# One more mirrored block of a symmetric score matrix turned by the DMA, and a third raw tile for V

## The chip, the cores and the metric

The kernel runs on one core of one Trainium2 chip. The metric is the device time of one launch in microseconds (us): the median of three runs of the kernel before is 2292.09 us (2291.48 to 2294.13). One further execution was taken with the profiler; all times inside the kernel come from it.

## The reference

Two stages follow each other. The first is an attention without softmax over 8 batches of 2496 rows; the second a mixture of 8 experts, in which each row goes to the one expert with the largest gate logit.

```
scores = (1/S) * z @ z.T              # per batch, S = 2496, z is [S, 64]
attn   = maximum(scores, 0) ** 2
x      = u * (attn @ v)               # v, u are [S, 256]
e      = argmax(x @ w_gate)           # per row, 8 experts
out    = softmax(x @ w_gate)[e] * (maximum(x @ w1[e], 0) @ w2[e])
```

`z @ z.T` is symmetric, and so is `attn`: the block of rows A and columns B is the transpose of the block of rows B and columns A.

## The kernel before, in words

**Tiling of the attention.** The 2496 rows of a batch are cut into five chunks of queries, 0 to 3 of 512 rows and 4 of 448. Keys go in ten pairs of 128-row tiles, `kp` = 0 to 9; two pairs make one chunk of keys, `cc = kp // 2`. A step is one (batch b, chunk c, pair kp). In each step `scores` (L255) makes a tile of 256 keys by up to 512 queries of `attn`, split into a rounded high part `hi` and a remainder `lo`, and `weighted` (L338) multiplies V into it: twelve matmuls of 128x128 by 128x512 (L346, L348, L349; V's high part by hi, V's high part by lo, V's low part by hi), ten in the last pair. `scores` of a step is written three steps ahead of its `weighted`. The order of a chunk's ten pairs comes from `order_of`.

**How a tile of scores comes about.** There are three ways.
- Blocks on or right of the diagonal (cc >= c) are computed: four matmuls (L309, L310) into PSUM, Relu and Square on ACT (L318, L319), the cast to `hi` (L320) and the subtraction to `lo` (L322) on DVE. Blocks right of the diagonal are also kept in one of six `slot` tiles, since they are needed again, mirrored, in chunk cc.
- Blocks left of the diagonal turned by TensorE: when the mirrored block is due, eight 128x128 float32 transposes per step (L281) bring it from the slot into PSUM, ACT copies it to `hi` (L282), DVE subtracts for `lo` (L283).
- Blocks left of the diagonal turned by the DMA: when the block is first computed (into a `tf` tile, of which there are three, rather than into the slot), ACT and DVE each copy one 16-bit half of every float into a `th` tile (L333, L334; three `th` tiles), and SyncE issues one DMA transpose of 512 KB from it into the slot (L335). When the mirrored block is due, ACT and DVE put the halves together again (L266, L267), and `hi` and `lo` are made from that (L268, L269).

`by_dma(c, cc)` (L251) chooses between the last two. Of the ten mirrored blocks of a batch, the four of chunk 4 go over TensorE, and of the other six that of chunks 0 and 3 does too; five go over the DMA. In chunk 3 the pairs 0 and 1 are that sixth block.

**Order within a chunk.** `order_of` (L228) lets the pairs right of the diagonal that the DMA will turn alternate with those that it won't. For chunk 0 of every batch but the first the order is 0, 2, 6, 3, 7, 4, 8, 5, 9, 1. Chunk 0 of the first batch goes in the natural order, 0 to 9.

**V.** A pair of V is fetched by SyncE into a `vr` tile (L137; two such tiles), then split into high and low parts by ACT (L142) and DVE (L143). The V of the next batch is fetched and split during chunk 4, one pair a step in the order in which the next chunk 0 will use them: `fetch_v` of place j and `split_v` of place j - 1 at step j (L877 to L883), the last split at the first step of the next chunk 0. In the first batch `fetch_v` runs two pairs ahead.

**What sets the order of instructions.** The program hands the instructions to a scheduler that plans each engine's order at compile time from the order in the source, dependences and free tiles. What is handed to `pinned` is kept behind the last instruction of each engine so far. Each engine, and SyncE with its DMA issues, then works through its list in order.

**Beside the steps.** At the end of a chunk `gate_x` (L363) forms x from the accumulators and splits it on DVE (L369, L379, L380); in the steps behind it a list of background work makes gate logits (L401), turns x into rows by four DMA transposes of 128 KB (L388, L389, L393), chooses experts, and stores rows and row lists. The experts' stage follows the attention (from about 1392 us in the trace; L779, L802, L805) and is not touched, but for one buffer count.

**Start.** The first matmuls only warm TensorE up: 8, then 4, then 8 of them read a tile named `lp` (L153). The tile `sd` holds raw integers for six constants (iota, L195, cast to float at L208), and later a block of the diagonal.

## Time and profile before

| | |
|---|---|
| median of three runs | 2292.09 us (2291.48 to 2294.13) |
| the profiled execution | 2294.91 us |
| its span, first to last instruction | 2293.2 us |
| granted TensorE clock, mean | 0.998 |
| PE, DVE, ACT busy | 2278.8, 1660.4, 1371.2 us |

The profile names engines PE (TensorE matmul), PEld (its weight loads), DVE (VectorE), ACT (ScalarE), POOL (GpSimd) and SP (SyncE, which issues most DMAs). L281 is line 281 of the kernel before. Matmuls overlap in the pipe, so the duration of one is longer than the distance to the next one; what a group of them costs the engine is read from the distance between starts. A name such as tf<-ps_s tells the tile written and the tile read.

The batches 2 to 6 look alike in the trace, about 172 us each. The part below uses batch 3: its chunks begin, by the first matmul of `weighted`, at 531.9, 569.1, 604.1, 636.4 and 671.5 us, and batch 4 begins at 704.0 us.

### The profile page before, as it was taken

The page shows a single profiled execution, that of the slowest core. Times are in us where ns is not written, and L with a number is a line of the kernel's source. Part 1 is how long each engine was busy: PE and PEld are TensorE (multiplying, and loading weights), DVE is VectorE, ACT ScalarE, POOL GpSimd, SP SyncE. Part 2 cuts the span into 40 slices and gives each one's busy share as a digit, 9 for nine tenths or more (in the row PEclk, how much of TensorE's full clock was granted, in tenths as well). Part 3 has the DMA queues.
Part 4 walks back from the last instruction along what each step waited for, and adds up shares of the span by engine and source line. Part 5 has one row for each costly group of instructions (what it writes and reads, how often), then busy time and mean ns, then how long its engine had stood idle before and what let it go on. Part 6 is the DMA issues. An engine that isn't in the chain of part 4 may idle for free.

```text
span 2293.2 us, 33793 instructions
## 1 busy us (share of the span) xinstructions
PE 2278.8 (99%) x12448; PEld 1937.2 (84%) x12448; DVE 1660.4 (72%) x2963; ACT 1371.2 (60%) x1867; POOL 614.3 (27%) x626
## 2 busy tenths in 40 slices
PE   9999999999999999999999999999999999999998
PEld 7888888888888888888888888888888888888887
DVE  8868868868878868868878867765575666657554
ACT  7747647647647647647647645454565655646554
POOL 1110110110110110110110244553454444445322
PEclk9999999999999999999999999999999999999999
DMA  5536635635626536635635668566667548557620
GB/s 154 102 65 119 117 60 122 119 60 121 119 61 121 119 60 121 120 58 123 120 62 100 111 136 181 153 149 155 158 184 155 178 129 202 142 147 193 154 88 29
DMA packets 421086, 278.92 MB, mean 122 GB/s; under 512 B 355820, under 2 KB 377850, under 8 KB 411696
## 3 DMA queue, kind: packets, MB, share of 16 engines
q1 hardware_dynamic: 389520, 157.59, 37.3%
q0 software_dynamic: 31392, 119.10, 18.1%
q8 instruction: 99, 1.62, 0.4%
q14 instruction: 75, 0.61, 0.1%
HBM read 149.79 MB, written 43.43 MB: 84 GB/s over the span
## 4 chain that ended last, share of the span: by engine, by line
PE 95%; ACT 1%; issue 1%; DMA 1%; DVE 1%; POOL 0%; SPq 0%; POOLq 0%; DVEq 0%; ACTq 0%
PE ph L779 19%; PE acc L349 15%; PE acc L346 15%; PE acc L348 14%; PE y L802 12%; PE y L805 6%; PE ps_s L309 4%; PE ps_s L310 4%; PE ps_s L281 3%; PE pt L401 1%; DMA vr<-in_v_dram 1%; PE ps_s L315 1%; ACT tf L319 0%; ACT tf L318 0%; POOL out_dram L818 0%
## 5 line engine op out<-in xcount | busy, mean ns | idle before, releaser
L349 PE MATMUL acc<-thi,t 128*128 128x512 f32 (+1 forms) x1600 | 615.2, 386 | 0.7 <-DVE t L143 0.7
L346 PE MATMUL acc<-thi,t 128*128 128x512 f32 (+1 forms) x1600 | 604.2, 392 | 0.0
L348 PE MATMUL acc<-tlo,t 128*128 128x512 f32 (+1 forms) x1520 | 585.8, 386 | 1.6 <-DVE tlo L322 1.6
L784 DVE SCALAR_TENSOR_TENSOR t<-ph,t 128x512 fp32r<-128x512 f32 (+1 forms) x328 | 221.3, 676 | 233.7 <-ACT t L783 230.8
L779 PE MATMUL ph<-thi,t 128*128 128x512 f32 (+2 forms) x1248 | 377.4, 360 | 0.0
L783 ACT ACTIVATE t<-ph 128x512 fp32r<-128x512 f32 (+1 forms) x328 | 193.3, 590 | 295.3 <-PE ph L779 283.5
L349 PEld LDWEIGHTS acc<-thi,t 128*128 128x128 f32 x1600 | 300.2, 188 | 56.3 <-DVE t L143 1.4
L346 PEld LDWEIGHTS acc<-thi,t 128*128 128x128 f32 x1600 | 299.6, 188 | 50.6
L348 PEld LDWEIGHTS acc<-tlo,t 128*128 128x128 f32 x1520 | 285.7, 188 | 53.5 <-DVE tlo L322 4.2
L479 POOL DMA_INDIRECT lst<-toks,posi x160 | 179.2, 1120 | 473.4 <-DVE posi L471 427.9
L802 PE MATMUL y<-t,t 128*128 128x512 f32 x1062 | 301.3, 392 | 0.0
L779 PEld LDWEIGHTS ph<-thi,t 128*128 128x128 f32 x1248 | 225.8, 189 | 27.6
L779 PE MATMUL ph<-tlo,t 128*128 128x512 f32 (+2 forms) x624 | 224.9, 360 | 0.0
L802 PEld LDWEIGHTS y<-t,t 128*128 128x128 f32 x1062 | 190.0, 188 | 31.6 <-issue 0.2
L818 POOL DMA_INDIRECT out_dram<-tf,lfidx x136 | 141.1, 1038 | 263.2 <-DVE tf L816 230.7
L805 PEld LDWEIGHTS y<-t,t 128*128 128x128 f32 x1062 | 174.2, 188 | 28.7
L805 PE MATMUL y<-t,t 128*128 128x256 f32 x1062 | 182.7, 280 | 0.0
L310 PE MATMUL ps_s<-t,t 128*128 128x512 f32 (+1 forms) x480 | 178.9, 376 | 0.0
L318 ACT ACTIVATE tf<-ps_s 128x1024 f32<-128x1024 f32 (+2 forms) x129 | 117.2, 909 | 76.7 <-PE ps_s L310 47.5
L383 POOL MEMSET rows<- 128x64 int32 x40 | 9.9, 251 | 557.0 <-DMA xrows<-rows 263.5
L714 POOL DMA_INDIRECT rows<-xrows,lfidx x136 | 142.7, 1049 | 57.0 <-issue 35.0
L320 DVE CAST thi<-tf 128x1024 fp32r<-128x1024 f32 (+2 forms) x129 | 79.5, 620 | 88.4 <-ACT tf L319 81.8
(251 smaller groups left out, 4032.9 us busy)
## 6 DMA issues: line engine op xcount, KB each, us to landing
vr<-in_v_dram SPq DMA_DIRECT2D x80, 256.0 KB
xrows<-rows SPq DMA_DIRECT2D x32, 544.0 KB
u<-in_ut_dram SPq DMA_DIRECT2D x32, 512.0 KB
zr<-in_zt_dram SPq DMA_DIRECT2D x38, 256.0 KB
u<-in_ut_dram SPq DMA_DIRECT2D x8, 448.0 KB
xrows<-rows SPq DMA_DIRECT2D x8, 408.0 KB
rows<-th SPq DMA_TRANSPOSE x160
lst<-toks,posi POOLq DMA_INDIRECT x160
```

What stands on the lines that cost most here:

```text
L310: nc.tensor.matmul(ps[:, i, m:n], lhsT=hl_k, rhs=lh_q[:, m:n], start=False, stop=True)
L346: nc.tensor.matmul(acc[d][:, :n], lhsT=vh, rhs=hi[:, i, :n], start=first and i == 0, stop=False)
L348: nc.tensor.matmul(acc[d][:, :n], lhsT=vh, rhs=lo[:, i, :n], start=False, stop=False)
L349: nc.tensor.matmul(acc[d][:, :n], lhsT=vl, rhs=hi[:, i, :n], start=False, stop=last and i == 1)
L479: i = nc.gpsimd.indirect_dma_start(out=lst1, out_offset=bass.IndirectOffsetOnAxis(ap=posi[:m, j:j + 1], axis=0), in_=toks[:m, col + j:col ...
L714: nc.gpsimd.indirect_dma_start(out=xg[:, s, :], out_offset=None, in_=src, in_offset=bass.IndirectOffsetOnAxis(ap=lists[which]["idx"][:, s, ...
L779: nc.tensor.matmul(o, lhsT=w1[:, part, dd, fs], rhs=xx[:, dd, :n], start=p == 0, stop=p == 5)
L783: nc.scalar.activation(hh[:, :m], ph[:, :m], AF.Relu)
L784: nc.vector.scalar_tensor_tensor(hl[:, :m], ph[:, :m], 0.0, hh[:, :m].bitcast(F32), op0=ALU.max, op1=ALU.subtract)
L802: nc.tensor.matmul(y, lhsT=h[:, cs], rhs=w2[:, f % 2].rearrange("p i d -> p (i d)"), start=f == 0, stop=False)
L805: nc.tensor.matmul(y[:, 0:D], lhsT=h[:, cs], rhs=w2[:, f % 2, 0, :], start=False, stop=f == NF - 1)
L818: d = nc.gpsimd.indirect_dma_start(out=out, out_offset=bass.IndirectOffsetOnAxis(ap=lists[which]["idx"][:, s, t:t + 1], axis=0), in_=yo[:, ...
```

## The change: what it does

It has four edits.
1. `by_dma` is true for chunks 0 and 3 as well: six of ten mirrored blocks are turned by the DMA.
2. In `order_of`, in chunk 0, three pairs that the DMA will turn come first, and only then do the two kinds alternate. The order becomes 0, 2, 3, 4, 5, 8, 6, 9, 7, 1.
3. `vr` gets a third tile (also where the tile lists of the experts' stage use that name). In chunk 4, step 0 fetches two places of the next batch's V and step j place j + 1; the splits stay where they were.
4. The warm-up matmuls read the `sd` tile, so the tile `lp` is gone. Its 2 KB per partition are the size of one `vr` tile.

```
-        vraw[b, kp] = sb.tile([P, 2, D], F32, name="vr", bufs=2)
+        vraw[b, kp] = sb.tile([P, 2, D], F32, name="vr", bufs=3)
...
-    warm = sb.tile([P, 2, QC], U16, name="lp", tag="lp")[:, 0].bitcast(BF16)
+    warm = ring_sd().rearrange("p s r -> p (s r)")[:, 0:QC // 2].bitcast(BF16)
...
-            mixed = []
+            mixed = [ways[0].pop(0) for _ in range(0 if c else 3)]
...
-        return c < cc < NC_ - 1 and (c, cc) != (0, 3)
+        return c < cc < NC_ - 1
...
-                r["tl", h] = sb.tile([P, 2, D], F32, name="vr", bufs=2).rearrange("p a d -> p (a d)")[:, 0:SMALL]
+                r["tl", h] = sb.tile([P, 2, D], F32, name="vr", bufs=3).rearrange("p a d -> p (a d)")[:, 0:SMALL]
...
-            fetch_v(b + 1, order_of(b + 1, 0)[j])
+            for i in ((0, 1) if j == 0 else (j + 1,) if j < NKP - 1 else ()):
+                fetch_v(b + 1, order_of(b + 1, 0)[i])
```

## The prediction

> **What bounds the kernel now.** I read the page first (engines, then the chain), then the groups of instructions, then the busy time by stretches of one batch.

> ```profile
> span 2293.2 us, 33793 instructions
> PE 2278.8 (99%) x12448; PEld 1937.2 (84%) x12448; DVE 1660.4 (72%) x2963; ACT 1371.2 (60%) x1867; POOL 614.3 (27%) x626
> PE 95%; ACT 1%; issue 1%; DMA 1%; DVE 1%; POOL 0%; SPq 0%; POOLq 0%; DVEq 0%; ACTq 0%
> ```

> PE is busy for 99% of the span and is 95% of the chain that ended last. A busy PE could still be a PE that waits a little, so the groups come next: busy, mean of one, then idle time before them and who ended it.

> ```profile
> L348 PE MATMUL acc<-tlo,t 128*128 128x512 f32 (+1 forms) x1520 | 585.8, 386 | 1.6 <-DVE tlo L322 1.6
> L281 PE MATMUL ps_s<-ident,s 128*128 128x128 f32 x640 | 86.0, 274 | 0.0
> L283 DVE TENSOR_TENSOR tlo<-ps_s,thi 128x896 fp32r<-128x896 f32 (+1 forms) x80 | 89.3, 1117 | 59.1 <-ACT thi L282 58.3
> L282 ACT CAST thi<-ps_s 128x896 fp32r<-128x896 f32 (+1 forms) x80 | 74.2, 928 | 111.9 <-PE acc L349 60.0 <-PE ps_s L281 51.8
> L266 ACT COPY tf<-s 128x1024 uint16<-128x1024 uint16 x80 | 105.2, 1359 | 13.7 <-DVE tlo L269 10.3 <-ACT thi L282 2.5 <-DMA s<-th 0.8
> L268 ACT CAST thi<-tf 128x1024 fp32r<-128x1024 f32 x80 | 82.7, 1052 | 59.9 <-PE acc L349 44.8 <-DVE tlo L269 8.8 <-DVE tf L267 4.2
> L267 DVE COPY tf<-s 128x1024 uint16<-128x1024 uint16 x80 | 57.7, 754 | 0.0
> L269 DVE TENSOR_TENSOR tlo<-tf,thi 128x1024 fp32r<-128x1024 f32 x80 | 97.8, 1223 | 32.4 <-ACT thi L268 31.1
> L333 ACT COPY th<-tf 128x1024 uint16<-128x1024 uint16 x80 | 83.9, 1049 | 0.7
> L334 DVE COPY th<-tf 128x1024 uint16<-128x1024 uint16 x80 | 55.2, 691 | 0.0
> ```

> The main matmuls hardly ever wait: the largest group that waits for DVE lost 1.6 us in the whole run. Work taken from PE in the attention should therefore shorten the run, as long as the work put on ACT, DVE and the DMA stays in their idle time. Where that idle time is, the five chunks of batch 3 show (stretch, length, then busy of PE, PEld, DVE, ACT, POOL, clock, DMA share, GB/s):

> ```profile
> 531.90:569.10 37.20, 37.20 (x193) 30.25 (x192) 31.63 (x53) 29.46 (x34) 5.30 (x5) 1.00 0.70 136
> 569.10:604.10 35.00, 35.00 (x185) 28.86 (x184) 30.37 (x59) 25.76 (x30) 5.37 (x5) 1.00 0.61 119
> 636.40:671.50 35.10, 35.10 (x206) 29.26 (x204) 25.53 (x47) 16.31 (x18) 6.07 (x7) 1.00 0.23 63
> 671.50:704.00 32.50, 32.50 (x196) 29.82 (x195) 21.40 (x34) 17.69 (x23) 2.29 (x4) 1.00 0.49 96
> 528.90:550.80 21.90, 21.90 (x123) 17.90 (x123) 21.62 (x40) 14.61 (x19) 2.00 (x2) 1.00 0.77 180
> 13.00:45.00 32.00, 31.83 (x140) 25.70 (x138) 29.48 (x43) 27.22 (x32) 0.00 (x0) 1.00 0.70 156
> ```

> PE is full in each. Chunk 3 (third row) has much room: ACT idles 18.8 us, DVE 9.6 us. Chunk 0 (first row) has little, and its first part (fifth row) none: DVE works 21.62 of 21.90 us there. Chunk 0 of batch 0 (last row) is nearly as tight. The change puts work into all three places, and that is the whole question.

> **The change part by part.** *Transposes on PE that go.* Two steps of chunk 3 in each of 8 batches lose their eight transposes: 16 groups, 128 of the 640 instructions. What a group costs PE is read from the chain, where each piece runs until the next begins.

> ```profile
> 627.04 0.87 PE ps_s L281 x8
> 632.00 0.23 PE acc L349
> ```

> A group advances PE by 0.87 us, a plain matmul by 0.23. So 16 x 0.87 = 13.9 us go from the engine that bounds the run. The row of 274 ns for one transpose is its time in the pipe; eight of them by that would be 2.2 us, not 0.87. [...]

> *Putting the block together in chunk 3.* Each of the 16 steps changes L282 and L283 for L266, L267, L268 and L269. ACT gets 1359 + 1052 - 928 = 1483 ns more, DVE 754 + 1223 - 1117 = 860 ns more; per chunk 3.0 us and 1.7 us. Six such steps then follow each other, each with only its twelve matmuls on PE, 12 x 0.23 = 2.8 us, against 2.4 us on ACT and 2.0 us on DVE, and `gate_x` besides. I cost it at nothing: it is covered by 18.8 us and 9.6 us of idle time, and ACT in that stretch waits for PE rather than the reverse, as in this row of the timeline:

> ```profile
> 641.82 1.05 ACT L268 CAST thi<-tf 128x1024 fp32r<-128x1024 f32 x1 [4.25 <-PE acc L349]
> ```

> Were that cover gone, it would cost up to 8 x 3.0 = 24 us.

> *Taking the halves in chunk 0.* Two more steps a batch run L333 (1.05 us on ACT), L334 (0.69 us on DVE) and one DMA transpose; Relu and Square are as long as before, only into `tf` rather than a slot. Per chunk 0 that is 2.1 us of ACT and 1.4 us of DVE, and by the new order four such steps stand among the first five in place of two. DVE decides. In batches 1 to 7 it has 5.6 us idle in the chunk, but 0.3 us in the first part, so taken alone the addition would cost PE between nothing (the idle time behind absorbs it) and 1.4 us a batch. Against it works the third edit. In that same first part DVE still splits four pairs of V:

> ```profile
> 528.90:550.80 21.90, 2.78 (x4) 1.00 0.77 180
> 507.83 3.86 SPq L137 DMA_DIRECT2D vr<-in_v_dram  x2
> 516.85 5.16 SPq L393 DMA_TRANSPOSE rows<-th  x4
> 522.11 1.00 SPq L137 DMA_DIRECT2D vr<-in_v_dram  x2
> 526.37 5.63 SPq L137 DMA_DIRECT2D vr<-in_v_dram  x3
> ACT t L142 <- DMA vr<-in_v_dram: 55.8, 20, 5.2
> 198.35 0.50 PE L348 MATMUL acc<-tlo,t 128*128 128x512 f32 x1 [1.42 <-DVE tlo L322]
> ```

> The first row is the busy time of L143 alone. They come so late because with two tiles a fetch waits for the split two places earlier, and SyncE, working in order, then stands in four transposes of rows for 5.2 us; ACT waits for V 20 times, 55.8 us in all. With three tiles each fetch can be issued one split sooner, ahead of those transposes, and the splits move into chunk 4, where DVE idles 11.1 us and ACT 14.8 us. I take two splits moved out of the first part: -2 x 0.69 against +2 x 0.69, net nothing, with +1.4 us a batch (no split moves) and -1.4 us (all four do) as ends. A gain beyond nothing can only come from waits that are there, and those are few: the 1.6 us above, nearly all of it at 198 us, in chunk 0 of batch 1 (last row).

> *SyncE and the DMA.* Each added transpose occupies SyncE and the rings; behind it in SyncE's list stand fetches of V, u and z and the stores of rows. For its price, the one transpose of the stretch from 560 to 569 us:

> ```profile
> 559.96 3.54 SPq L335 DMA_TRANSPOSE s<-th  x1
> q1 hardware_dynamic: 2526, 0.63, 76.8%
> GB/s 224 177 17 10 7 72 85 38 26 38 30 74 10 33 93 155 284 289 291 290 291 265 74 0 0 0 0 0 0 0 0 0 0 0 0 0 0 0 0 0
> ```

> At the top rate, some 290 GB/s, 0.52 MB take 1.8 us; by the share of the stretch (76.8% of 9 us for 0.63 MB, some of it rows) 5.7 us. I take 3.5 us, SyncE's own time on it. Two more bring chunk 0 from 0.70 x 37.2 = 26.0 us of DMA to 33.0, under 37.2, so I cost it at nothing; u, z and the rows have until the end of the chunk, and V will have been fetched earlier. If that cover is gone, ACT stands before a `th` tile still being read (second rival). [...]

> *Chunk 0 of batch 0.* Pairs 6 and 7 gain the halves in natural order, and no split of V can move to an earlier chunk. DVE has 2.5 us idle in 32 and ACT is held by V behind SyncE's transposes:

> ```profile
> 31.03 2.88 SPq L335
> 34.01 3.00 DMA vr<-in_v_dram
> 37.04 0.62 ACT t L142
> ```

> The third tile lets V be fetched a step sooner, which answers the two transposes more in SyncE's list. I take the DVE work at full price, 1.4 us; the ends are 0 and, if V comes late by one SyncE transpose and its landing, 2.9 + 3.0 = 5.9 us.

> *The start.* The constants' integers share a tile with the warm-up, so POOL's iota and DVE's casts wait for warm-up matmuls. Now they lie in DVE's wait for the first z:

> ```profile
> 1.69 0.10 DVE L208 CAST e_down<-sd 128x8 f32<-128x8 int32 x1
> 3.63 0.51 DVE L130 CAST t<-x 64x512 fp32r<-64x512 f32 x1 [0.39 <-DMA x<-in_zt_dram]
> 4.31 0.20 DVE L208 CAST tno<-sd 128x23 f32<-128x23 int32 x1
> ```

> From 1.69 on, and again up to 4.51, they take some 2.0 us. Moved behind, they fall into the tight first chunk: between 0 and 2.0 us; I take 1.0.

> *Sum.* -13.9 + 0 (chunk 3) + 0 (chunks 0 of batches 1 to 7) + 1.4 + 1.0 = -11.5 us. The profiled execution took 2294.9 us, 2.8 above the median; -11.5 gives 2283.4 on it and 2280.6 on the median. The terms' ends: with nothing at the start and in batch 0 and the 1.6 us of waits gone, 2292.1 - 13.9 - 1.6 = 2276.6; with 5.9, 2.0 and half of the 1.4 us in seven chunks (4.9), 2291.0. A measurement of this kernel tells about 0.2%, 4.6 us, from no change.

> **The rivals.** *DVE becomes the bound of chunk 0.* If the third tile brings no split forward, every chunk 0 pays 1.4 us: -13.9 + 8 x 1.4 + 1.0 = -1.7, so 2290.4, no change. For it speaks the full fifth row above, and that the only DVE wait is there; against it the 5.6 us idle in the same chunk and the plain reason why the splits are late. 0.15.

> *The DMA jams and ACT stands (slower).* Four transposes now follow each other step by step, and `th` has three tiles, which the row transposes use too. A tile comes free when its transpose has landed. At 5.7 us each, four take 22.8 us; the four steps take 4 x 16 x 0.23 = 14.7 us on PE, so the last tile comes free 8.1 us late. The lead of three tiles, less the one in work, hides about one step, 3.7 us. ACT, which works in order, would hold back the scores behind L333 for 4.4 us in each chunk 0: 8 x 4.4 = 35 us, 2292.1 - 11.5 + 35 = 2316. It decides from the point where a transpose amid the other traffic takes over 4.6 us ((14.7 + 3.7) / 4). For it: a DMA share of 0.77 in the first part; against it: 3.5 us on SyncE, and no ACT wait for `th` among the waits now. 0.09.

> *V's earlier splits do more.* If all four leave the first part, DVE gains 1.4 us a batch there, the 1.6 us wait goes and batch 0 is relieved as well: 2276.6 or a little less. PE has nothing more to give. 0.12.

> *A transpose costs PE its 274 ns.* Then 128 x 0.274 = 35.1 us go, 2292.1 - 35.1 + 2.4 = 2259.4. The chain's row is against it. 0.01. [...]

> **How the numbers follow.** The forecast, 2280.6, has 0.63 with its own range of 2277 to 2285. The rivals hold 0.15, 0.09, 0.12 and 0.01. From 2276.5 to 2291 lie the forecast, most of the third rival, and the first: about 0.8 once the forecast's own misses are allowed for. Faster by over 0.2% (under 2287.5): 0.63 + 0.12 + 0.01, and 0.01 of the first rival, less 0.02 for an order of instructions that the planner lays worse: 0.75. Within 0.2%: 0.15. Slower: 0.10.

> **What would show it.** Right: L281 x512 with no other PE group grown; L266 to L269, L333 and L334 x96; chunk 3 shorter by 1.7 us, chunk 0 unchanged at 37.2 us; L143 in its first part x2 and ACT's wait for V well under 55.8 us; DMA share of chunk 0 near 0.89. Wrong: PE groups L346 or L348 idle for DVE by over 5 us (first rival), ACT L333 waiting for the DMA (second), or chunk 3 no shorter although its transposes are gone.

## The result, and the profile after

| | before | after |
|---|---|---|
| median of six runs each on one chip | 2293.57 us (2291.48 to 2297.8) | 2318.56 us (2313.47 to 2322.51) |
| ratio, 95% interval | | 1.0106 [1.0096, 1.0116] |
| span of the profiled execution | 2293.2 us | 2316.2 us |
| granted clock, mean | 0.998 | 0.994 |
| attention ends (last matmul of `weighted`) | 1391.0 us | 1413.3 us |

The change makes the kernel 1.06% slower; 2280.6 us was predicted. Nearly all of the loss lies in the attention, which is 22.3 us longer in the profiled execution; the experts' stage takes 902.2 us before and 902.9 after. Up to L878 the line numbers are those of before.

The page of the changed kernel, head and chain:

```profile
span 2316.2 us, 33703 instructions
PE 2277.0 (98%) x12320; PEld 1929.0 (83%) x12320; DVE 1672.9 (72%) x2995; ACT 1399.1 (60%) x1899; POOL 617.3 (27%) x626
PE 89%; DVE 5%; issue 2%; ACT 1%; DMA 1%; SPq 0%; POOL 0%; DVEq 0%; POOLq 0%; ACTq 0%
```

PE is no busier, and 6 points less of the chain: DVE now holds 5% of it. The groups of the changed kernel (busy, mean of one, idle before them and its cause) say where:

```profile
L348 PE MATMUL acc<-tlo,t 128*128 128x512 f32 (+1 forms) x1520 | 590.9, 390 | 20.2 <-DVE tlo L322 20.2
L346 PE MATMUL acc<-thi,t 128*128 128x512 f32 (+1 forms) x1600 | 603.5, 393 | 2.9 <-DVE thi L320 2.9
L281 PE MATMUL ps_s<-ident,s 128*128 128x128 f32 x512 | 69.8, 274 | 0.0
L333 ACT COPY th<-tf 128x1024 uint16<-128x1024 uint16 x96 | 100.5, 1047 | 1.0
L334 DVE COPY th<-tf 128x1024 uint16<-128x1024 uint16 x96 | 65.9, 687 | 0.3
```

The counts are those predicted (L281 x512, L333 and L334 x96), so the change does what it says. The matmuls that wait for `tlo`, 1.6 us before, wait 20.2 us. Three stretches of batch 3 in the changed kernel, with the columns of the prediction's rows (chunk 0, chunk 3, then chunk 0's first part), and what PE waited for in its chunk 0 (in all, times, longest):

```profile
534.20:577.80 43.60, 39.73 (x192) 31.19 (x192) 32.45 (x54) 30.57 (x36) 4.01 (x5) 0.96 0.65 134
645.10:678.40 33.30, 33.30 (x198) 27.91 (x197) 25.66 (x50) 15.21 (x18) 8.00 (x7) 1.00 0.33 74
531.20:553.10 21.90, 19.12 (x103) 15.20 (x102) 18.29 (x35) 13.11 (x15) 1.03 (x2) 0.92 0.83 187
```

```profile
PE acc L348 <- DVE tlo L322: 2.8, 2, 2.6
PE ps_s L309 <- ACT s L318: 0.6, 2, 0.4
PE acc L346 <- DVE thi L320: 0.5, 1, 0.5
```

Chunk 3 went from 35.10 to 33.30 us with PE still full: the gain came. Chunk 0 went from 37.20 to 43.60; PE, which waited for nothing there before, idles 3.9 us in it, and the granted clock falls to 0.96. Added up over the batches, from the starts of the first matmul of `weighted` in each chunk:

| | before | after | |
|---|---|---|---|
| start of batch 0's chunk 0 | 12.8 us | 11.2 | -1.6 |
| chunk 0 of batch 0 | 36.6 | 36.3 | -0.3 |
| chunk 0 of batches 1 to 7 | 261.1 | 301.3 | +40.2 |
| chunk 3 of all batches | 281.2 | 265.7 | -15.5 |
| chunks 1, 2 and 4 of all batches | 799.2 | 798.9 | -0.3 |

The chain in batch 3's chunk 0 of the changed kernel (start, length, what) shows one such loss whole:

```profile
545.43 0.60 DVE thi L320
546.04 0.60 DVE th L334
546.64 0.33 DVE t L129
...
547.00 0.43 DVE t L130
...
547.46 1.24 DVE tlo L322
548.69 0.04 issue
548.74 0.50 PE acc L348
...
551.59 0.43 PE acc L346
...
553.35 0.23 PE acc L348
```

VectorE works without a pause through a list that ends in the remainder `tlo`; the matmul that needs it has waited 2.6 us. Then the matmuls come 0.43 us apart rather than 0.23 for some 4 us. Two further waits follow at 559 and 560 us, when the scores of pair 8 come late. What became of V, in the changed kernel's waits and in the busy time of L143 alone in the first part:

```profile
ACT t L142 <- DMA vr<-in_v_dram: 0.8, 1, 0.8
531.20:553.10 21.90, 2.30 (x4) 0.92 0.83 187
```

ScalarE's wait for V fell from 55.8 us to 0.8, as forecast, and yet the stretch still holds four splits (x4, as before). Three of them lie in the chunk in both kernels. The first lies just ahead of it, and is the one that moved: it starts 3.4 us before the chunk rather than 0.9 (in batches 4 and 7 it stood at 3.1 and 3.3 already), so a part of it falls out of the stretch (2.30 us in place of 2.78).

### The profile page after: what moved, and what is told of

It reads as the page before. It is cut to its first block, busy times and chain, and to the rows that moved or that the text cites. A ratio compares the mean times of both kernels' runs of the same rounds, so it can differ in the third digit from the quotient of the medians.

```text
span 2316.2 us, 33703 instructions
## 1 busy us (share of the span) xinstructions
PE 2277.0 (98%) x12320; PEld 1929.0 (83%) x12320; DVE 1672.9 (72%) x2995; ACT 1399.1 (60%) x1899; POOL 617.3 (27%) x626
## 3 DMA queue, kind: packets, MB, share of 16 engines
q1 hardware_dynamic: 422800, 165.98, 39.8%
## 4 chain that ended last, share of the span: by engine, by line
PE 89%; DVE 5%; issue 2%; ACT 1%; DMA 1%; SPq 0%; POOL 0%; DVEq 0%; POOLq 0%; ACTq 0%
PE ph L779 19%; PE acc L349 14%; PE acc L346 14%; PE acc L348 13%; PE y L802 12%; PE y L805 6%; PE ps_s L309 4%; PE ps_s L310 4%; PE ps_s L281 2%; DVE tlo L322 1%; DVE thi L320 1%; PE pt L401 1%; DVE th L334 1%; DMA th<-sd 1%; DVE t L143 1%
## 5 line engine op out<-in xcount | busy, mean ns | idle before, releaser
L349 PE MATMUL acc<-thi,t 128*128 128x512 f32 (+1 forms) x1600 | 618.2, 388 | 0.0
L348 PE MATMUL acc<-tlo,t 128*128 128x512 f32 (+1 forms) x1520 | 590.9, 390 | 20.2 <-DVE tlo L322 20.2
L346 PE MATMUL acc<-thi,t 128*128 128x512 f32 (+1 forms) x1600 | 603.5, 393 | 2.9 <-DVE thi L320 2.9
L346 PEld LDWEIGHTS acc<-thi,t 128*128 128x128 f32 x1600 | 302.0, 189 | 57.7 <-DVE thi L320 5.4
L348 PEld LDWEIGHTS acc<-tlo,t 128*128 128x128 f32 x1520 | 287.6, 189 | 74.5 <-DVE tlo L322 24.7
L349 PEld LDWEIGHTS acc<-thi,t 128*128 128x128 f32 x1600 | 302.3, 189 | 55.8 <-DVE t L143 0.6
L479 POOL DMA_INDIRECT lst<-toks,posi x160 | 187.9, 1174 | 429.7 <-DVE posi L471 384.2
L318 ACT ACTIVATE tf<-ps_s 128x1024 f32<-128x1024 f32 (+2 forms) x145 | 133.4, 924 | 110.7 <-PE ps_s L310 74.8
L805 PEld LDWEIGHTS y<-t,t 128*128 128x128 f32 x1062 | 174.2, 188 | 30.4 <-DVE t L784 1.9
L805 PE MATMUL y<-t,t 128*128 128x256 f32 x1062 | 182.7, 280 | 1.4 <-DVE t L784 1.4
L714 POOL DMA_INDIRECT rows<-xrows,lfidx x136 | 142.2, 1046 | 66.5 <-issue 37.3
L320 DVE CAST thi<-tf 128x1024 fp32r<-128x1024 f32 (+2 forms) x145 | 90.4, 627 | 95.7 <-ACT tf L319 90.0
```

Of the source, the lines that this page charges most:

```text
L346: nc.tensor.matmul(acc[d][:, :n], lhsT=vh, rhs=hi[:, i, :n], start=first and i == 0, stop=False)
L348: nc.tensor.matmul(acc[d][:, :n], lhsT=vh, rhs=lo[:, i, :n], start=False, stop=False)
L349: nc.tensor.matmul(acc[d][:, :n], lhsT=vl, rhs=hi[:, i, :n], start=False, stop=last and i == 1)
L479: i = nc.gpsimd.indirect_dma_start(out=lst1, out_offset=bass.IndirectOffsetOnAxis(ap=posi[:m, j:j + 1], axis=0), in_=toks[:m, col + j:col ...
L714: nc.gpsimd.indirect_dma_start(out=xg[:, s, :], out_offset=None, in_=src, in_offset=bass.IndirectOffsetOnAxis(ap=lists[which]["idx"][:, s, ...
L805: nc.tensor.matmul(y[:, 0:D], lhsT=h[:, cs], rhs=w2[:, f % 2, 0, :], start=False, stop=f == NF - 1)
```

## The experiments

The kernels ran on several chips. On two of them (that of e1, e6, e8 and e9, and that of e2, e16, e17 and e18) the kernel before itself took 2342.7 and 2340.0 us; in the kernels traced there the more is in the experts' stage (930 to 954 us). There the ratio to before and the lengths of chunks are what to read, and those hardly depend on the chip: chunk 1 is 34.9 us in nearly every trace. Lengths in us, chunk 0 of batches 2 to 6 and chunk 3 as means. Some of these chunks 0 hold a fall of the clock (mean 0.96 over the chunk in batch 3 of the changed kernel and in batch 5 of e17), worth 1.3 to 1.7 us: four of the five in the changed kernel, two in e17, one each in e1 and e9, none in the other rows.

| kernel | chunk 0 of batch 0 | of batch 1 | of 2 to 6 | chunk 3, mean | ratio to before |
|---|---|---|---|---|---|
| before | 36.6 | 38.6 | 37.1 | 35.1 | 1 |
| after | 36.3 | 42.9 | 43.3 | 33.2 | 1.0106 [1.0096, 1.0116] |
| e1 block alone | 38.3 | 43.2 | 39.8 | 33.2 | 1.0044 [1.0018, 1.0071] |
| e2 order alone | 36.4 | 42.3 | 37.6 | 35.1 | 1.0021 [1.0001, 1.0041] |
| e3 V and warm-up alone | 35.8 | 37.2 | 37.0 | 35.1 | 1.0006 [0.9997, 1.0016] |
| e17 VectorE's copies alone | 36.7 | 43.7 | 40.0 | 35.1 | 1.0095 [1.0064, 1.0125] |
| e18 ScalarE's copies alone | 36.9 | 39.3 | 37.1 | 35.1 | 1.000 [0.9975, 1.0025] |
| e20 block, low halves on ScalarE | 39.1 | 37.6 | 38.5 | 33.2 | 0.9982 [0.9973, 0.9991] |
| e21 as e20, with V | 36.2 | 37.1 | 38.8 | 33.2 | 0.9981 [0.9972, 0.9990] |
| e9 pair 8 later | 36.3 | 41.0 | 39.7 | 33.9 | 0.9989 [0.9954, 1.0023] |
| e15 and V split earlier | 36.2 | 38.9 | 38.8 | 33.2 | 0.998 [0.997, 0.999] |
| e16 and z split later | 36.4 | 40.2 | 40.8 | 33.3 | 0.9997 [0.9978, 1.0015] |

The theory at the outset: VectorE's list in the first part of chunk 0 is too long, and pair 8, whose z is split in it, stands one place too early. The rivals: the DMA and its `th` tiles; the clock as a cost of its own; V.

**Is it the DMA?** The changed kernel, in which pairs 4 and 5 of chunk 0 take their halves in idle slots, so that five `th` tiles serve rather than three:

```
+            if b and c == 0 and kp in (4, 5):
+                th = slot(free[3 - kp])[:, 0:2 * QC].bitcast(U16).rearrange("p (i h n) -> p i h n", i=2, h=2)
+            else:
+                th = ring_halves().rearrange("p (i h) n -> p i h n", h=2)
```

> The changed kernel, but in chunk 0 of batches 1 to 7 the halves of pairs 4 and 5 are put into slots that are free at that time, so that five th tiles are at hand rather than three. Theory C: the waiting goes, 2278 to 2290 us. Theories A and B: no change, 2315 to 2322 us.

Chunk 0 stayed at 43.3 us, ratio 1.012 [1.0032, 1.0207]. PE's wait in its batch 3, beside the changed kernel's 2.8, is

```profile
PE acc L351 <- DVE tlo L322: 2.8, 2, 2.6
...
PE acc L349 <- DVE thi L320: 0.5, 1, 0.5
```

the same to the tenth. The number of `th` tiles is not the cause; nor does ScalarE wait for one at L333 anywhere in the changed kernel.

**The parts alone.** First the block, in the order of before and with two V tiles:

```
-        return c < cc < NC_ - 1 and (c, cc) != (0, 3)
+        return c < cc < NC_ - 1
...
+            if c == 0:
+                mixed = [2, 6, 3, 7, 4, 8, 5, 9]
             for i, kp in zip(at, mixed):
```

> The kernel before with the sixth block turned by the DMA and nothing else: chunk 0 stays in the order 0, 2, 6, 3, 7, 4, 8, 5, 9, 1, two raw V tiles, the warm-up tile as before. Theory A: pair 8 stands where it stood, so the 13.9 us of transposes come off almost whole: 2278 to 2286 us. Theory B: five steps with halves in a row and no third V tile, 2315 us or more. Theory C: the same, 2318 us or more.

Chunk 0 39.8 us, with a wait of 1.6 us for `tlo` in batch 3, and slower than before: the block alone loses more than it gains. Batch 0, without the third V tile, is 1.7 us longer than before. Then the order alone (the edit of `mixed` from the change, nothing else):

> The kernel before with the second edit alone: chunk 0 goes 0, 2, 3, 4, 5, 8, 6, 9, 7, 1; pairs 6 and 7 are still turned by TensorE in chunk 3, V has two tiles. Theory that pair 8 stands one place too early, since the z of the last chunk is split only in step 1: chunk 0 grows by the 3.6 us that moving pair 8 back gained, perhaps less as VectorE has 1.4 us less to do, so 39.5 to 41 us, ScalarE waits about 12 us for one scores matmul rather than 7, ratio 1.007 to 1.012. Rival that the order costs only together with the halves of four pairs in a row: chunk 0 within 0.5 us of 37.1, ratio 0.999 to 1.002.

37.6 us. That refutes half of the theory: the order by itself costs 0.5 us in batches 2 to 6, not 3.6. In batch 1 it costs 3.7 us (42.3 in place of 38.6, with a wait of 3.5 us for `tlo`), and there the kernel before already waits 1.4 us. So it seems to cost where VectorE is late already. Then the third V tile, its fetches and the warm-up edit alone:

> The kernel before with the third V tile, its fetches and the warm-up edit alone; five blocks by the DMA, order of before. Theory that this edit moves no split, since the splits are tied to their place in the order of the program: VectorE's L143 at the same places of chunk 0, chunk 0 37.0 to 37.2 in batches 2 to 6, ratio 0.999 to 1.001, though ScalarE's wait for V (55.8 us before) is gone. Rival, the step of the prediction: two splits leave the first part, chunk 0 is not longer and VectorE idles 1.4 us more in it.

Chunk 0 37.0 us, the four splits still in the first part. Busy time of L143 alone there, and its places, in this kernel, whose chunk 0 starts at 527.13:

```profile
524.10:546.00 21.90, 2.32 (x4) 1.00 0.74 168
```

```profile
523.69 0.69 DVE L143 TENSOR_TENSOR t<-vr,t 128x512 fp32r<-128x512 f32 x1
533.08 0.68 DVE L143 TENSOR_TENSOR t<-vr,t 128x512 fp32r<-128x512 f32 x1
533.88 0.68 DVE L143 TENSOR_TENSOR t<-vr,t 128x512 fp32r<-128x512 f32 x1
538.80 0.68 DVE L143 TENSOR_TENSOR t<-vr,t 128x512 fp32r<-128x512 f32 x1
```

An earlier fetch took no split out of the chunk: three lie in it as before, and the first, ahead of it, moved by 2.5 us in this batch. What the edit gives is in batches 0 and 1, whose chunks 0 shorten by 0.8 and 1.4 us; the whole time does not show it. In its profiled execution the experts' stage takes 908.3 us rather than 902.2, with a new wait of 3.4 us for VectorE at L805.

**Which engine's copies?** Now the halves of pairs 6 and 7 in chunk 0 of batches 1 to 7, on one engine at a time, with no transpose and no other edit. On VectorE:

```
+        elif b and c == 0 and cc == 3:
+            th = ring_halves().rearrange("p (i h) n -> p i h n", h=2)
+            src = a.bitcast(U16).rearrange("p i (n h) -> p i n h", h=2)
+            nc.vector.tensor_copy(th[:, :, 1, :], src[:, :, :, 0])
         return hi, lo
```

> The kernel before, with one addition: in chunk 0 of batches 1 to 7, VectorE alone also copies the low halves of pairs 6 and 7 into a th tile that nobody reads (L334, 0.69 us each); ScalarE copies nothing more, no transpose is issued, the mirrored block of chunk 3 still goes over TensorE. Theory that the rest of the loss in chunk 0 is VectorE's work in its first part: chunk 0 grows from 37.1 us to between 38.5 and 39.8, with a PE wait for a tlo tile of 1 to 2 us; 7 x 1.4 to 7 x 2.7 us, ratio 1.004 to 1.008. Rival that it is ScalarE's copies or the transposes' DMA time: chunk 0 stays within 0.3 us of 37.1 and the ratio is 1.000 to 1.001.

On ScalarE, the last line being `nc.scalar.copy(th[:, :, 0, :], src[:, :, :, 1])`:

> The mirror of the run with VectorE's copies: the kernel before, with ScalarE alone copying the high halves of pairs 6 and 7 in chunk 0 of batches 1 to 7 (L333, 1.05 us each) into a th tile that nobody reads; VectorE does nothing more and no transpose is issued. Theory that VectorE is what fills the first part: chunk 0 within 0.3 us of 37.1, ratio 1.000 to 1.001. Rival that ScalarE's 2.1 us are the cost: chunk 0 38.5 us or more, ratio 1.004 or more. If neither this nor VectorE's copies move chunk 0, the transposes' DMA time is left.

VectorE's copies alone bring chunk 0 to 40.0 us, as long as with the whole block (39.8); ScalarE's leave it at 37.1. Where the clock held, it is 39.2 to 39.5 us with VectorE's copies and 39.2 to 39.7 with the block. The clearest pair of the study: two copies of 0.69 us on one engine are enough for the whole loss of the block, with no transpose issued. In the mean the two copies, 1.2 us of VectorE's list (their starts to the next), cost 2.9 us, and 2.1 to 2.4 where the clock held. Why it is more than 1.2, the timelines show. VectorE in batch 3 of the kernel before, whose chunk 0 starts at 531.89 (rows between are left out):

```profile
542.73 1.24 DVE L322 TENSOR_TENSOR tlo<-tf,thi 128x1024 fp32r<-128x1024 f32 x1
543.87 0.70 DVE L334 COPY th<-tf 128x1024 uint16<-128x1024 uint16 x1
...
546.37 0.42 DVE L129 CAST t<-zr 64x512 fp32r<-64x512 f32 x1
546.82 0.42 DVE L130 CAST t<-zr 64x512 fp32r<-64x512 f32 x1
```

and in the kernel with VectorE's copies (L339), whose chunk 0 starts at 538.68:

```profile
541.50 0.69 DVE L339 COPY th<-s 128x1024 uint16<-128x1024 uint16 x1
...
549.24 0.68 DVE L339 COPY th<-s 128x1024 uint16<-128x1024 uint16 x1
549.84 0.41 DVE L129 CAST t<-zr 64x512 fp32r<-64x512 f32 x1
550.28 0.42 DVE L130 CAST t<-zr 64x512 fp32r<-64x512 f32 x1
...
551.59 0.69 DVE L334 COPY th<-tf 128x1024 uint16<-128x1024 uint16 x1
552.19 1.22 DVE L322 TENSOR_TENSOR tlo<-tf,thi 128x1024 fp32r<-128x1024 f32 x1
```

The third remainder starts 10.8 us after the chunk in the one, 13.5 in the other: 2.7 us later. Two copies are 1.2 of that. The rest are an L334 (0.6) and the two casts of z (0.9), which came behind the remainder and now come ahead of it. The scheduler planned another order for VectorE, and what it put ahead of the awaited remainder counted: PE waits 1.7 us for it there, and 0.6 us for another result of VectorE just before. In the changed kernel the same remainder starts at 547.46, 13.2 us after 534.22.

**The converse.** The block alone again, the low halves of pairs 6 and 7 copied by ScalarE:

```
+            if b and c == 0 and cc == 3:
+                nc.scalar.copy(th[:, :, 1, :], src[:, :, :, 0])
+            else:
+                nc.vector.tensor_copy(th[:, :, 1, :], src[:, :, :, 0])
```

> The block of chunks 0 and 3 turned by the DMA, alone, in the order of before with two V tiles (that variant had chunk 0 at 39.8 us), and in chunk 0 of batches 1 to 7 ScalarE rather than VectorE copies the low halves of pairs 6 and 7: VectorE has nothing more to do than before, ScalarE 4 x 1.05 us more, the transposes are all there. Theory that VectorE's place in the list is the whole of the loss: chunk 0 back to 37.0 to 37.5, chunk 3 33.2, so 8 x 1.85 = 14.8 us less than before but for up to 3 us in chunk 0, ratio 0.9935 to 0.996. Rival that the transposes or ScalarE, now with 4.2 us more, hold up the scores: chunk 0 38.5 to 40 us, ratio 0.998 to 1.004.

Ratio 0.9982 [0.9973, 0.9991], 2286.35 us beside 2291.91: faster than before by 0.2%. Chunk 0 is 38.5, so 1.3 of the 2.7 us are gone and not all of them, as the theory had it. In its batch 3 the third remainder starts 11.0 us after the chunk (537.03 and 526.04), nearly as in before; what is late next is ScalarE, which VectorE now waits for. PE's one wait in that chunk, 0.8 us, is for the split of z (L132) that VectorE makes behind this:

```profile
537.03 1.21 DVE L324 TENSOR_TENSOR tlo<-tf,thi 128x1024 fp32r<-128x1024 f32 x1
...
541.90 0.69 DVE L322 CAST thi<-tf 128x1024 fp32r<-128x1024 f32 x1 [1.05 <-ACT tf L321]
```

With the third V tile and its fetches as well, and each V split one step earlier (`split_v` of place j at step j, none left to chunk 0):

> As the run with ScalarE's low halves, with the third V tile, its earlier fetches and the warm-up edit of the change, and each split of V one step earlier (none left in chunk 0); order of before. Theory that V's splits count only through VectorE's first part, which is full but no longer late: chunk 0 36.8 to 37.3, batch 1's chunk 0 shorter by the wait for V, ratio within 0.001 of the other run. Rival that the splits taken out of chunk 0 are worth their 0.6 us each: chunk 0 36 us or less and 5 us more gained. Rival that the order planned for VectorE comes out worse: chunk 0 38 to 39 us.

Ratio 0.9981 [0.9972, 0.9990], the same. Batch 0's chunk 0 is 2.9 us shorter than without the V tile (39.1 to 36.2), and those of batches 2 to 6 0.3 us longer, where 36.8 to 37.3 us was expected.

**The order within the changed kernel.** Pair 8 moved back one place (`mixed = [2, 3, 4, 5, 6, 8, 7, 9]`):

> The changed kernel, but chunk 0 in the order 0, 2, 3, 4, 5, 6, 8, 7, 9, 1: pair 8, whose keys are the last chunk's and whose z is split only in the second step of chunk 0, goes back from the sixth place to the seventh, where it stood before. Theory A (pair 8 stands too early: its scores can't start before z is split, the scores behind it queue, TensorE runs out of prepared steps and waits, and its clock falls): one more step is prepared early, the waits of TensorE in chunk 0 (2.6 us at one place) go, chunk 0 is back to about 37.2 us and the run takes 2278 to 2286 us. Theory B (VectorE has too much to do in the first part of chunk 0): five steps with halves now stand in a row, so the waits stay or grow, 2315 to 2330 us. Theory C (the DMA transposes in a row jam the th tiles): five in a row, 2318 us or more.

Chunk 0 39.7 us, ratio 0.9989 [0.9954, 1.0023]. One wait is left, and the two late ones for pair 8's scores are gone. PE's waits in its chunk 0 of batch 3:

```profile
PE acc L350 <- DVE tlo L324: 1.7, 1, 1.7
```

The same with the splits of V one step earlier, as above:

> The changed kernel with pair 8 in the seventh place, and each split of V one step earlier in the program (place j at step j of chunk 4, none in chunk 0). Theory B': one split of V, 0.6 us, leaves the first part, so chunk 0 takes 38.5 to 39.3 us; ratio 0.996 to 0.999. Theory E (what a third raw tile was thought to do: several splits leave the first part): 37.2 us, ratio 0.994.

38.8 us, ratio 0.998 [0.997, 0.999]; a version that beats before. PE still waits 1.35 us for `tlo` in batch 3. And with z split in step 2 rather than 1 on top (`ZF, ZS = (0, 2), (2, 4)`):

> The faster variant so far (all four edits, pair 8 moved back to the seventh place, V split one step earlier; chunk 0 38.8 us) with one thing more: the z of the last chunk is split in step 2 of chunk 0 rather than in step 1, since pair 8 in the seventh place needs it only from step 3 on. Theory that what is left of chunk 0's loss is VectorE's work ahead of the fourth remainder: the 1.74-us wait shrinks by the 0.8 us of the two casts of z that stood ahead of it, chunk 0 37.9 to 38.2 us, time 4 to 6 us less than the variant without it, ratio 0.995 to 0.997. Rival that z then comes too late for pair 8's scores: chunk 0 39 to 43 us, ratio 0.999 to 1.010. Rival that VectorE's order is not what the wait hangs on: chunk 0 38.8, ratio 0.998.

40.8 us, longer against the expectation: the casts of z left the place ahead of the remainder, but pair 8's scores then came late. PE's waits in its batch 3:

```profile
PE acc L350 <- DVE tlo L324: 1.7, 2, 1.2
PE acc L348 <- DVE thi L322: 0.5, 1, 0.5
PE ps_s L311 <- ACT s L320: 0.2, 1, 0.2
```

The other direction, z earlier in the changed kernel (fetched in chunk 4, split in step 0 of chunk 0):

> The changed kernel, but the last chunk's z of the next batch is fetched in chunk 4 (eighth step) and split in the first step of chunk 0, not the second. Theory A: pair 8 is free one step sooner, so part of the waiting goes, 2290 to 2312 us. Theory B: VectorE has the z split 1.4 us earlier in its fullest part, so no better, 2316 to 2325 us. Theory C: no change, 2316 to 2321 us.

Chunk 0 42.1, ratio 1.0034 [1.0007, 1.0061]: the 2.6-us wait for `tlo` stays, the late ones are gone. The means differ by 1.2 us, but here the clock fell in every one of these batches, in two of them for twice as long (in batch 3 its mean over the chunk is 0.92, in the changed kernel's 0.96). With one fall on both sides chunk 0 goes from 43.5 to 43.7 us to 41.6 to 41.7. So z's time is worth some 1.9 us, by way of the late waits. The diagonal's pair 1 as fourth (0, 2, 3, 1, 4, 5, 8, 6, 9, 7), a pair without halves among those with:

> The changed kernel with chunk 0 of batches 1 to 7 in the order 0, 2, 3, 1, 4, 5, 8, 6, 9, 7: the pair on the diagonal, which needs no halves and only half the scores, splits the row of steps with halves, and pair 8 is in the seventh place. Theory B': VectorE has 1.3 us less in the first part than with five steps with halves in a row, so chunk 0 takes 37.2 to 39 us; ratio 0.993 to 0.998. Rival D: 39.5 us or more.

Chunk 0 40.1 (38.9 to 39.6, in one batch 43.3), ratio 1.0006 [0.9996, 1.0015].

**GpSimd instead of VectorE.** The order with pair 8 later, and the low halves of pairs 2 to 5 in chunk 0 copied by GpSimd:

> The changed kernel with pair 8 in the seventh place, as in the run before, and with the copy of the low halves of pairs 2 to 5 in chunk 0 of batches 1 to 7 (0.69 us each on VectorE) moved to GpSimd. Theory B' (what pair 8 doesn't explain, 2.6 us a chunk 0, is VectorE's work in the first part): four copies, 2.8 us, leave VectorE there, so the last wait in chunk 0 goes and it takes 37.0 to 37.6 us in place of 39.7; ratio to the kernel before 0.993 to 0.996. Rival D (the wait comes from the way the scores are queued, or the clock, not from VectorE): chunk 0 stays at 39 us or more, ratio 0.998 or more.

Chunk 0 43.2, ratio 1.0068 [1.0051, 1.0086], longer against the expectation. GpSimd takes 1.49 us for a copy; the last two transposes of chunk 0's first part are issued 18.1 us after its start rather than 14.8 (with the copies on VectorE), and then ScalarE does stand before a `th` tile. ScalarE's row, and the chain, of this kernel in batch 3:

```profile
559.33 1.05 ACT L335 COPY th<-tf 128x1024 uint16<-128x1024 uint16 x1 [4.50 <-DMA s<-th]
```

```profile
546.79 12.44 DMA s<-th
...
559.25 0.04 DVE th L336
...
559.86 1.23 DVE tlo L324
```

So the second rival's mechanism exists, once copies are slower; in the changed kernel it isn't at work.

**The clock.** The changed kernel, with twelve matmuls of 128x384 that nothing reads, put where PE waits for the remainder:

```
+            if c == NC_ - 1 and b + 1 < B:
+                for k in range(12):
+                    nc.tensor.matmul(pt[:, 128:QC], lhsT=ones, rhs=top(x)[:, 0, 0:384], start=k == 0, stop=k == 11,
+                                     skip_group_check=True)
```

> The changed kernel with twelve matmuls more on TensorE behind the gate logits of chunk 4's rows, ahead of the place where it waits 2.6 us in chunk 0 of batches 1 to 7; nothing reads their result. If the wait drops the clock (the eight matmuls behind it start 0.43 us apart, not 0.23), some 2 us of matmuls in the wait cost nothing and keep the clock: chunk 0 goes from 43.3 to 41 to 42 us. If the spacing has another cause, chunk 0 stays at 43.3 us or grows by up to 2 us.

Chunk 0 42.0 in place of 43.3 us, ratio 1.0092 [1.0072, 1.0112]. In batch 1 PE waits 3.1 us as before and the clock falls as before, and chunk 0 is 2.0 us longer. The four us after the wait, in the changed kernel and then in this one (stretch, length, PE, PEld, DVE, ACT, POOL, clock, DMA, GB/s):

```profile
549.30:553.30 4.00, 4.00 (x12) 3.12 (x11) 2.13 (x4) 0.00 (x0) 1.23 (x2) 0.57 1.08 270
```

```profile
549.30:553.30 4.00, 3.94 (x17) 3.29 (x18) 2.76 (x7) 0.00 (x0) 0.90 (x1) 1.00 0.98 224
```

Clock 0.57 with 12 matmuls against 1.00 with 17. In two of the changed kernel's batches (5 and 7) the clock held by itself, and their chunks 0 are 42.0 too, where those of batches 2, 3, 4 and 6 are 43.5 to 43.7. So the fall of the clock is shown, and its price in these batches is 1.5 to 1.7 us.

## Why the prediction was wrong

**Right:** the gain in chunk 3, and that the work added there hides: -15.5 us measured against -13.9, PE full as before. A group of eight transposes was worth 15.5 / 16 = 0.97 us, not the 2.2 of their 274 ns each. The DMA, costed at nothing, shows no part in the loss; its share of chunk 0 is 0.65, not 0.89, that is 28.3 us beside 26.0: with two transposes more and one fetch of V less in the chunk it grew by 2.3 us rather than 7.0.

**The step that failed** is that of chunk 0: "I take two splits moved out of the first part: -2 x 0.69 against +2 x 0.69, net nothing." The first half did not happen: no split left the chunk. The splits are `pinned` to their place in the program's order, behind the scores of the step they stand in; the late fetch made ScalarE wait, but did not set the splits' place in VectorE's order within the chunk. Third tile or not, L143 comes four times in the first part (the run of that edit alone). Taking the wait away moved one split by up to 2.5 us, ahead of the chunk, and none out of it. The second half was mis-sized: the copies are 1.2 us of VectorE, but 2.1 to 2.4 us of chunk 0 when put in by themselves (2.9 in the mean, with falls of the clock), as the planned order put more ahead of the awaited remainder. And the cover named in the prediction, 5.6 us of idle VectorE in the chunk, lies behind the remainder and could give nothing to it: in batch 3 of before VectorE works without a break from the chunk's start to 550.8 us, and the third remainder starts at 542.73.

**Not seen at all** were two followers of that wait. In the changed order pair 8 stands one place earlier, its scores need the z that VectorE splits late, and short waits follow, some 1.2 us by the trace and 1.9 by the run with z earlier. And after the wait of 2.6 us the clock took some 1.6 us more, in four of the six batches 2 to 7. Batch 3 by its trace: 2.6 (the wait), 1.6 (the clock), 1.2 (pair 8) and 0.7 in two shorter gaps between matmuls make 6.1 of the 6.4.

**Rivals.** The first named the right place, the right engine and the right condition (no split brought forward), and its sign came: L348 idle for VectorE by 20.2 us. Its price was 1.4 us a chunk in place of 5.7 (40.2 / 7), because it priced only the copies. The third, with all four splits gone from the first part, fell with the same step. The second gave 2316, nearly the result, by another cause: with five `th` tiles nothing changed. A number that fits is no evidence for its mechanism.

**Batch 0 and the start**, +1.4 and +1.0, came out at -0.3 and -1.6. In batch 0 the third tile is worth 0.8 us alone (36.6 to 35.8) and 2.9 with the block (39.1 to 36.2); the sum gave it too little. The start can't be judged: five other kernels with the start of before (e1, e2, e17, e18, e20) begin batch 0's chunk 0 between 11.0 and 13.4 us, so it moves by more than the term.

**Open:** what is left of chunk 0's loss in the best versions (1.3 to 1.7 us; in e15 still a wait for `tlo`, in e20 and e21 waits that differ by batch), and why the plan puts z ahead. The three faster versions keep 0.2% of the 0.7% that chunk 3 offers (15.5 of 2293 us).

## What to carry to other kernels

Find the one instruction that the bounding engine awaits, and count what stands ahead of it in the other engine's list; idle time behind it is no cover. Taking away a wait moves work only if that wait set the work's place; where program order pins it, look at the pin. And after any edit to a planned kernel compare the order on the tight engine, since the plan can put more ahead of the awaited instruction than the edit added.

## What the runs showed of the hardware

After PE had waited 2.6 us for `tlo` in batch 3, the granted clock was 0.57 over the next 4 us; such a fall came in four of the six batches 2 to 7, and in the other two (5 and 7) the clock held after the same wait. With VectorE's copies alone the clock fell in batch 5, behind waits of 0.7 and 1.7 us (0.75 from 901.5 to 906.5 us, chunk 0 of 41.1 us), and held in batch 3, behind waits of 0.6 and 1.7 us (1.00 from 550.5 to 556.5 us, chunk 0 of 39.4).

```profile
545.97:549.38 3.41, 0.78 (x9) 0.59 (x6) 3.35 (x8) 0.00 (x0) 0.00 (x0) 1.00 1.14 211
549.38:552.80 3.42, 3.42 (x10) 2.64 (x9) 2.05 (x4) 0.00 (x0) 0.97 (x1) 0.50 1.10 264
```

```profile
897.46:900.87 3.41, 2.21 (x32) 1.66 (x30) 3.38 (x10) 0.76 (x1) 0.00 (x0) 1.00 0.89 232
900.87:904.29 3.42, 1.99 (x9) 1.65 (x10) 3.36 (x7) 0.00 (x0) 0.00 (x0) 1.00 1.10 201
904.29:907.70 3.41, 3.41 (x17) 2.83 (x16) 0.73 (x2) 0.00 (x0) 1.92 (x2) 1.00 1.02 310
```

PE idles 2.6 us of the one stretch, and 1.2 and 1.4 us of the two. In the chunks 0 of the changed kernel's batches 1 to 7, the five stretches ahead of a fall hold 2.06 to 2.63 us of idle PE; of the other stretches at a clock of 1.00 none holds more than 1.80 us (from 1252.5 us, batch 7). So in this trace the fall went with idle time inside one stretch, not with the length of the wait; where between 1.80 and 2.06 us it begins to come, and why, the trace does not show.
